# Output weights at sixteen SBUF start addresses modulo 512 bytes, in a kernel bound by TensorE

## The chip, the core and the metric

The kernel runs on one core of a Trainium2 chip. The metric is the device time of one execution in microseconds (us), as the median of several runs. Beside it stands one execution recorded by the hardware profiler; its span runs from the first to the last instruction.

## What is computed

Three blocks follow each other: attention with a causal mask and a cumulative bias (4 x 8 heads, 576 positions, head size 64), a gated product block, and a feed-forward block. The change touches the last one, on 2304 tokens:

```python
def _moe2_ref(x, w_in, w_out) -> np.ndarray:   # x 2304x512, w_in 512x2048, w_out 2048x512
    h = x @ w_in
    g = h - np.tanh(h)
    return (g @ w_out).astype(np.float32)
```

## The kernel before

The kernel keeps the accuracy of wide operands by splitting each one in two float32r tiles, a high part (names that end in h) and a low part (names in l). A product is then three matmuls: high by high, high by low, low by high.

All work is first written down as operations with their tiles, and a planner (`Plan`) puts them in an order by their assumed durations and priorities; tiles are then placed in pools on the left or the right side of SBUF, in the order in which they are listed. A tile that lies over one that was released waits for that tile's last users, and for no others. The planner knows nothing of addresses.

The last stage works through the tokens in five blocks `HT` of 512 columns (the last has 256). For each block and each of sixteen groups f of 128 hidden features it does the following:

- L945: twelve matmuls, weights `wih` and `wil`, moving operand `x2b`, up to 512 columns, into a PSUM bank.
- L953 to L960: ScalarE (ACT) and VectorE (DVE) make g from it, in `u`, `sq`, `th`, `pg`, `mk`.
- L396 (DVE) or L395 (ACT) writes the high part `gh`; L401 (GpSimd, POOL) writes the low part `gl`. These lines are those of the helpers `copy` and `sub`.
- L966 to L968: for each 128 tokens n of the block three matmuls that accumulate over f in bank n. The stationary operand (the weight that is loaded into the array) is a 128-column piece of `gh` or `gl`; the moving operand is the whole of `voh[f]`, `vol[f]`, `voh[f]`, 512 columns each.

`voh[f]` and `vol[f]` are the two parts of 128 rows of `w_out`, one pair for each f, 2048 bytes per partition and tile. The first four pairs are in pool `pre`, on the left behind `wih` and `wil`; their values come back from DRAM by a DMA (`fetch`, tile `wt_d`), while the stage before still runs. The other twelve pairs are in pool `p2`, on the right, and are made by `convert`: DMA into `wraw`, some steps on ACT and DVE in `wt`, a copy into `voh` and a subtraction into `vol`. `p2` lies over the tiles of the stage before: `wah`, `wal`, `woh`, `wol`, the input ring `cf`, and `x2s`, from which that stage's result is stored to DRAM and read back as `x2b`.

In the built program all the large tiles of this stage start at 480 modulo 512 bytes: `wih`, `wil`, `x2b`, `gh`, `gl`, and every `voh` and `vol`. In the attention stage the tiles `kh`, `kl` and `qs`, `q2` start at 480 or 224, and a piece that begins at column 288 of `kh` or `kl` therefore at 96 or 352.

Of the kernel before, what the change touches and what calls it, by code (L numbers as in the profile page):

```python
# [10 lines left out]
F32R = mybir.dt.float32r  # L11
# [5 lines left out]
P = 128  # L17
# [3 lines left out]
DM, DF, DF2 = 512, 1024, 2048  # L21
KC = DM // P
NF = DF // P
NF2 = DF2 // P
# [307 lines left out]
def tile_kernel(ctx, tc, qk, v, s, w1, w2, w3t, w_out, w_in, w_out2, out):  # L332
    nc = tc.nc
# [35 lines left out]
    bank = []  # L369
# [21 lines left out]
    def dma(dst, src, nbytes, r, w, prio, row=4096, issue=450.0, rate=320.0):  # L391
        pl.op([("SP", issue, lambda: nc.sync.dma_start(dst(), src()))], r=r, w=w, prio=prio, xfer=max(nbytes / rate, nbytes / row * 4.0))

    def copy(dst, src, n, r, w, prio, psum=False):
        pl.op([("ACT", c_act(n, psum), lambda: nc.scalar.activation(dst(), src(), AF.Copy)),  # L395
               ("DVE", c_dve(n, not psum), lambda: nc.vector.tensor_copy(dst(), src()))], r=r, w=w, prio=prio, two=not psum, kind="copy")  # L396
# [7 lines left out]
    def split(hi, hb, lo, lb, src, n, r, prio, psum=False):  # L404
        copy(hi, src, n, r, [hb], prio, psum)
        sub(lo, src, hi, n, r + [hb], [lb], prio, psum)
# [7 lines left out]
    def pe(mms, fn, r, w, prio):  # L414
        pl.op([("PE", c_mms(mms), fn)], r=r, w=w, prio=prio, mms=mms)
# [58 lines left out]
    NPRE = PARAM["npre"]  # L474
    pre = Pool("pre", "left")
    p2 = Pool("p2", "right")
    voh = [(pre if f < NPRE else p2).buf(f"voh{f}", [P, DM], F32R) for f in range(NF2)]
    vol = [(pre if f < NPRE else p2).buf(f"vol{f}", [P, DM], F32R) for f in range(NF2)]
    x2b = [q_.buf(f"x2b{i}", [P, 2, KC, BLK], F32R) for i, q_ in enumerate((pre, p2))]
    gh_r = p2.ring("gh", PARAM["ng"], [P, BLK], F32R)  # L480
    gl_r = p2.ring("gl", PARAM["ng"], [P, BLK], F32R)
# [8 lines left out]
    def assemble(src, prio, first=None, after=()):  # L490
        r_, t_ = raw_r.next(), t1_r.next()
        h32, l32 = (lambda: r_.t[:, :, 1]), (lambda: r_.t[:, :, 0])
        tf = lambda: t_.t.bitcast(F32)
        dma(lambda: r_.t, lambda: src.bitcast(U32).rearrange("p (n t) -> p n t", t=2), P * 4096, list(after), [r_], prio if first is None else first)
        pl.op([("ACT", c_act(512), lambda: nc.scalar.activation(tf(), h32().bitcast(F32), AF.Abs)),  # L495
               ("DVE", c_dve(512, True), lambda: nc.vector.tensor_scalar(t_.t, h32(), 0x7FFFFFFF, None, op0=ALU.bitwise_and))], r=[r_], w=[t_], prio=prio, two=True, kind="copy")
        dve(lambda: nc.vector.tensor_scalar(tf(), tf(), HI_CLAMP, LO_CLAMP, op0=ALU.min, op1=ALU.max), 512, [t_], [t_], prio, fast=True)
        dve(lambda: nc.vector.tensor_scalar(t_.t, t_.t, 3, 0x3FFFFFF8, op0=ALU.logical_shift_left, op1=ALU.bitwise_and),
            512, [t_], [t_], prio, fast=True)
        dve(lambda: nc.vector.scalar_tensor_tensor(t_.t, h32(), 0xC0000000, t_.t, op0=ALU.bitwise_and, op1=ALU.bitwise_or),  # L500
            512, [r_, t_], [t_], prio, two=True)
        dve(lambda: nc.vector.scalar_tensor_tensor(t_.t, l32(), 29, t_.t, op0=ALU.logical_shift_right, op1=ALU.bitwise_or),
            512, [r_, t_], [t_], prio, two=True)
        return t_

    def convert(src, hi, hb, lo, lb, prio, first=None, after=()):
        t_ = assemble(src, prio, first, after)
        split(hi, hb, lo, lb, lambda: t_.t.bitcast(F32), 512, [t_], prio)
# [5 lines left out]
    def fetch(i, hi, hb, lo, lb, prio, first=None):  # L514
        dma(lambda: lo().bitcast(F32), lambda: wt_d.t[i], P * 2048, [(wt_d, i)], [lb], prio if first is None else first)
        copy(hi, lambda: lo().bitcast(F32), 512, [lb], [hb], prio)
        sub(lo, lambda: lo().bitcast(F32), hi, 512, [hb], [lb], prio)
# [60 lines left out]
    for e in e2[:1] + [None] + e2[1:]:  # L578
        if e is None:
            zero([lambda: ssum.t], [20], [ssum], -5, 1.0)  # L580
            for R in rqk:
                a = 0 if R is rqk[0] else S
# [8 lines left out]
    for t, (q0, q1) in enumerate(QT):  # L591
        a, o = ROFF[t]
# [331 lines left out]
    raw_r.bufs, t1_r.bufs = raw[:2], bit[:2]  # L924
    for f in range(NF2):
        if f in lay:
            fetch(f, lambda f=f: voh[f].t, voh[f], lambda f=f: vol[f].t, vol[f], 3.5e5 + 10 * f, PARAM["layf"])
        else:
            convert(w_out2[f * P:(f + 1) * P, :], lambda f=f: voh[f].t, voh[f], lambda f=f: vol[f].t, vol[f], 3.5e5 + 10 * f)
    h_ring = Ring(bank[BLK // P:8])  # L930
    for j, (t0, t1) in enumerate(HT):
        w = t1 - t0
        X2 = x2b[j % 2]
        js = range(t0 // 512, (t1 - 1) // 512 + 1)
        dma(lambda X2=X2, w=w: X2.t[:, :, :, :w].bitcast(F32), lambda t0=t0, t1=t1: x2_d.t[:, :, :, t0:t1], P * 8 * w * 4,
            [(x2_d, [i * KC + d for i in js for d in range(KC)])], [X2], 3.0e5)
        for f in range(NF2):
            pos = (j * NF2 + f) * 10.0
            bk = h_ring.next()

            def mm(bk=bk, X2=X2, f=f, w=w):
                a = slice(f * P, (f + 1) * P)
                for k in range(KC):
                    for n, (w_, i) in enumerate(((wih, 0), (wih, 1), (wil, 0))):
                        nc.tensor.matmul(bk.t[:, :w], w_.t[:, k, a], X2.t[:, i, k, :w], start=k == 0 and n == 0, stop=k == KC - 1 and n == 2)  # L945
            parts = [k * 4 + f // 4 for k in range(KC)]
            pe(12 * f_mm(w), mm, [X2, (wih, parts), (wil, parts)], [bk], 2.0e6 + pos)
            u, sq, th, pg, mk = u_r.next(), sq_r.next(), th_r.next(), pg_r.next(), mk_r.next()
            gh, gl = gh_r.next(), gl_r.next()
            hp = lambda bk=bk, w=w: bk.t[:, :w]  # L950
            c_ = lambda x, w=w: x.t[:, :w]
            pr = 3.0e5 + pos
            act(lambda u=u, hp=hp, c_=c_: nc.scalar.activation(c_(u), hp(), AF.Square), w, [bk], [u], pr, psum=True)  # L953
            act(lambda u=u, sq=sq, c_=c_: nc.scalar.activation(c_(sq), c_(u), AF.Square, bias=const.t[:, 0:1], scale=SQ_A), w, [u, const], [sq], pr, extra=93.0)
            act(lambda th=th, hp=hp, c_=c_: nc.scalar.activation(c_(th), hp(), AF.Tanh), w, [bk], [th], pr, psum=True)
            dve(lambda u=u, pg=pg, hp=hp, c_=c_: nc.vector.tensor_tensor(c_(pg), hp(), c_(u), op=ALU.mult), w, [bk, u], [pg], pr)  # L956
            dve(lambda sq=sq, pg=pg, c_=c_: nc.vector.scalar_tensor_tensor(c_(pg), c_(sq), SQ_K, c_(pg), op0=ALU.add, op1=ALU.mult), w, [sq, pg], [pg], pr, two=True)
            act(lambda u=u, mk=mk, c_=c_: nc.scalar.activation(c_(mk), c_(u), AF.Relu, bias=const.t[:, 1:2]), w, [u, const], [mk], pr, extra=93.0)  # L958
            dve(lambda th=th, hp=hp, c_=c_: nc.vector.tensor_tensor(c_(th), hp(), c_(th), op=ALU.subtract), w, [bk, th], [th], pr)
            dve(lambda pg=pg, mk=mk, th=th, c_=c_: nc.vector.copy_predicated(c_(pg), c_(mk).bitcast(U32), c_(th)), w, [mk, th], [pg], pr, two=True)  # L960
            copy(lambda gh=gh, c_=c_: c_(gh), lambda pg=pg, c_=c_: c_(pg), w, [pg], [gh], pr)
            sub(lambda gl=gl, c_=c_: c_(gl), lambda pg=pg, c_=c_: c_(pg), lambda gh=gh, c_=c_: c_(gh), w, [pg, gh], [gl], pr, psum=t1 == NT and f >= NF2 - 2)
            for n in range(w // P):
                def om(n=n, f=f, gh=gh, gl=gl):
                    a = slice(n * P, (n + 1) * P)
                    nc.tensor.matmul(bank[n].t, gh.t[:, a], voh[f].t, start=f == 0, stop=False)  # L966
                    nc.tensor.matmul(bank[n].t, gh.t[:, a], vol[f].t, start=False, stop=False)  # L967
                    nc.tensor.matmul(bank[n].t, gl.t[:, a], voh[f].t, start=False, stop=f == NF2 - 1)  # L968
                pe(3 * f_mm(512), om, [gh, gl, voh[f], vol[f]], [bank[n]], 2.0e6 + pos + PARAM["outlag"] + n)
        for n in range(w // P):  # L970
            ob = osb_r.next()
            for a, z in ((0, 256), (256, 512)) if t1 == NT else ((0, 512),):
                copy(lambda ob=ob, a=a, z=z: ob.t[:, a:z], lambda n=n, a=a, z=z: bank[n].t[:, a:z], z - a, [bank[n]], [(ob, int(a > 0))] if t1 == NT else [ob], 3.0e5 + j * 160, psum=True)
            dma(lambda t0=t0, n=n: out[t0 + n * P:t0 + (n + 1) * P, :], lambda ob=ob: ob.t, P * DM * 4, [ob], [], 0)
# [46 lines left out]
```

## Time and profile before

| | us |
|---|---|
| median of 3 runs | 932.16 (930.49 to 932.52) |
| the profiled execution, its own time | 931.48 |
| its span | 929.8 |
| TensorE (PE) busy | 921.6 |
| DVE busy | 700.5 |
| ACT busy | 426.6 |
| POOL busy | 377.8 |

The execution's own time is 1.7 us longer than the span of its instructions. PE's busy time is made of modelled ends of overlapping matmuls; how long a matmul really holds the engine is read from the distance between the starts of two that follow each other.

### The profile page before, as it was taken

How to read it: one execution, taken by the hardware profiler on the slowest of the kernel's cores; microseconds unless marked ns; L12 is line 12 of the kernel's file. 1: busy time of each engine (PE TensorE's matmuls, PEld its weight loads, DVE VectorE, ACT ScalarE, POOL GpSimd, SP SyncE). 2: the span in 40 equal slices, each digit the busy share in tenths (PEclk: the TensorE clock that was granted, in tenths of full speed). 3: DMA queues.
4: the chain of work that ended last, by engine and by line, in shares of the span. 5: the costliest groups of instructions: out<-in, count | busy, mean ns of one | idle time of the engine just before them, and what ended most of it. 6: DMA issues, size and time to landing. Idle time of an engine off the chain costs nothing.

```text
span 929.8 us, 14217 instructions
## 1 busy us (share of the span) xinstructions
PE 921.6 (99%) x5007; PEld 765.1 (82%) x5007; DVE 700.5 (75%) x1485; ACT 426.6 (46%) x952; POOL 377.8 (41%) x309
## 2 busy tenths in 40 slices
PE   9999999999999999999999999999999999999998
PEld 7777878888887888899888988888888888888887
DVE  8999897876664299996789999997556655656665
ACT  7857565655551022211423275554444444444353
POOL 2256765545342044414978544452222222222221
PEclk9999999999999999999999999999999999999999
DMA  7666646654421144477897652221020001100010
GB/s 226 183 199 181 201 146 205 213 160 135 131 84 49 56 147 155 164 233 240 284 326 247 227 176 68 75 107 46 1 91 15 31 1 46 46 1 0 1 47 23
DMA packets 58888, 115.36 MB, mean 124 GB/s; under 512 B 5713, under 2 KB 24305, under 8 KB 58818
## 3 DMA queue, kind: packets, MB, share of 16 engines
q1 hardware_dynamic: 58818, 114.47, 38.6%
q8 instruction: 39, 0.64, 0.3%
q14 instruction: 31, 0.25, 0.1%
HBM read 85.30 MB, written 25.46 MB: 119 GB/s over the span
## 4 chain that ended last, share of the span: by engine, by line
PE 92%; DVE 4%; POOL 1%; issue 1%; ACT 1%; DMA 1%; POOLq 0%; DVEq 0%
PE bank L945 21%; PE bank L806 20%; PE bank L966 7%; PE bank L967 7%; PE bank L968 7%; PE bank L725 5%; PE bank L752 4%; PE bank L908 4%; PE bank L909 4%; PE bank L907 4%; PE bank L670 2%; PE bank L671 2%; PE bank L668 2%; PE bank L872 1%; PE bank L871 1%; PE bank L870 1%
## 5 line engine op out<-in xcount | busy, mean ns | idle before, releaser
L401 POOL TENSOR_TENSOR gl<-pg,gh 128x512 fp32r<-128x512 f32 (+1 forms) x78 | 99.2, 1272 | 260.9 <-DVE gh L396 249.0
L945 PE MATMUL bank<-x2b,wih 128*128 128x512 f32 (+1 forms) x640 | 181.3, 368 | 0.0
L945 PEld LDWEIGHTS bank<-x2b,wih 128*128 128x128 f32 x640 | 117.0, 188 | 21.2
L958 ACT ACTIVATE mk<-u,const 128x512 f32<-128x512 f32 (+1 forms) x80 | 54.5, 681 | 142.5 <-DVE pg L960 142.4
L945 PE MATMUL bank<-x2b,wil 128*128 128x512 f32 (+1 forms) x320 | 117.7, 368 | 0.0
L966 PE MATMUL bank<-voh,gh 128*128 128x512 f32 x288 | 112.2, 390 | 0.0
L967 PE MATMUL bank<-vol,gh 128*128 128x512 f32 x288 | 112.2, 390 | 0.0
L968 PE MATMUL bank<-voh,gl 128*128 128x512 f32 x288 | 112.0, 389 | 0.0
L691 ACT ACTIVATE e<-e,nmx 128x576 f32<-128x576 f32 (+4 forms) x160 | 89.2, 559 | 39.7 <-DVE nmx L685 38.8
L956 DVE TENSOR_TENSOR pg<-bank,u 128x512 f32<-128x512 f32 (+1 forms) x80 | 50.9, 636 | 42.3 <-POOL gl L401 42.3
L685 DVE CUSTOM_DVE_ANT_0 e<-bank,msk 128x288 f32<-128x288 f32 (+4 forms) x160 | 64.3, 422 | 16.5 <-PE bank L671 14.2
L725 PE MATMUL bank<-ident,e 128*128 128x128 f32 (+1 forms) x480 | 75.4, 276 | 0.6 <-ACT e L691 0.3
L396 DVE CAST gh<-pg 128x512 fp32r<-128x512 f32 (+1 forms) x77 | 30.5, 396 | 52.8 <-PE bank L967 52.6
L945 PEld LDWEIGHTS bank<-x2b,wil 128*128 128x128 f32 x320 | 60.3, 188 | 9.9
L401 POOL TENSOR_TENSOR xl<-cf,xh 128x512 fp32r<-128x512 f32 (+1 forms) x40 | 53.3, 1360 | 34.2 <-DVE xh L396 32.3
L953 ACT ACTIVATE u<-bank 128x512 f32<-128x512 f32 (+1 forms) x80 | 43.7, 546 | 50.4 <-PE bank L945 42.3
L395 ACT ACTIVATE en<-bank 128x256 f32<-128x256 f32 (+3 forms) x97 | 40.9, 427 | 52.2 <-PE bank L725 42.3
L495 ACT ACTIVATE wt<-wraw 128x512 f32<-128x512 f32 x54 | 36.4, 673 | 59.4 <-DMA wraw<-w_in 26.7
L968 PEld LDWEIGHTS bank<-voh,gl 128*128 128x128 f32 x288 | 54.1, 188 | 11.4
L966 PEld LDWEIGHTS bank<-voh,gh 128*128 128x128 f32 x288 | 54.2, 188 | 10.8
L967 PEld LDWEIGHTS bank<-vol,gh 128*128 128x128 f32 x288 | 54.1, 188 | 10.5
L806 PE MATMUL bank<-xh,w1h 128*128 128x512 f32 (+1 forms) x160 | 62.7, 392 | 0.0
(134 smaller groups left out, 2280.2 us busy)
## 6 DMA issues: line engine op xcount, KB each, us to landing
rqk<-qk SPq DMA_DIRECT2D x24, 576.0 KB
wraw<-w_out SPq DMA_DIRECT2D x24, 512.0 KB
wraw<-w SPq DMA_DIRECT2D x16, 512.0 KB
c_d<-cst SPq DMA_DIRECT2D x32, 256.0 KB
wraw<-w3t SPq DMA_DIRECT2D x16, 512.0 KB
wraw<-w_in SPq DMA_DIRECT2D x16, 512.0 KB
cf<-c_d SPq DMA_DIRECT2D x32, 256.0 KB
x_d<-x2s SPq DMA_DIRECT2D x16, 512.0 KB
```

Source lines behind the costliest of these rows:

```text
L401: o.append(("POOL", c_pool2(n), lambda: nc.gpsimd.tensor_tensor(dst(), a(), b().bitcast(F32), op=ALU.subtract)))
L685: nc.vector.tensor_tensor_reduce(e.t[:nq, EOFF[t] + k0:EOFF[t] + k1], bk.t[:nq, :k1 - k0], bi.t[:nq, bo + k0:bo + k1], -0.125, 3.0e38 if f ...
L691: act(lambda: nc.scalar.activation(et(), et(), AF.Exp, bias=nmx.t[:nq, i, tm:tm + 1], scale=-1.0, accum_out=ssum.t[:nq, pj, t, i:i + 1]), ...
L725: nc.tensor.transpose(bk.t[:rows, (at + m) * P:(at + m + 1) * P], e.t[:, EOFF[t] + c * P:EOFF[t] + c * P + rows], ident.t)
L806: nc.tensor.matmul(bk.t[:, :w], w_.t[:, k, f * P:(f + 1) * P], x_.t[:, k, :w], start=k == 0 and i == 0, stop=k == KC - 1 and i == 2)
L945: nc.tensor.matmul(bk.t[:, :w], w_.t[:, k, a], X2.t[:, i, k, :w], start=k == 0 and n == 0, stop=k == KC - 1 and n == 2)
L953: act(lambda u=u, hp=hp, c_=c_: nc.scalar.activation(c_(u), hp(), AF.Square), w, [bk], [u], pr, psum=True)
L956: dve(lambda u=u, pg=pg, hp=hp, c_=c_: nc.vector.tensor_tensor(c_(pg), hp(), c_(u), op=ALU.mult), w, [bk, u], [pg], pr)
L958: act(lambda u=u, mk=mk, c_=c_: nc.scalar.activation(c_(mk), c_(u), AF.Relu, bias=const.t[:, 1:2]), w, [u, const], [mk], pr, extra=93.0)
L966: nc.tensor.matmul(bank[n].t, gh.t[:, a], voh[f].t, start=f == 0, stop=False)
L967: nc.tensor.matmul(bank[n].t, gh.t[:, a], vol[f].t, start=False, stop=False)
L968: nc.tensor.matmul(bank[n].t, gl.t[:, a], voh[f].t, start=False, stop=f == NF2 - 1)
```

## The change

Each of the 32 tiles becomes 128 columns (512 bytes) wider, and its 512 columns of data begin at column 8f, so 32f bytes behind the tile's start. `wo2` makes that view, and all writers and readers use it. `voh[f]` and `vol[f]` have the same f and so the same offset; their data start at 480 + 32f modulo 512: 480 for f = 0, 0 for f = 1, 32 for f = 2, up to 448 for f = 15.

```diff
-    voh = [(pre if f < NPRE else p2).buf(f"voh{f}", [P, DM], F32R) for f in range(NF2)]
-    vol = [(pre if f < NPRE else p2).buf(f"vol{f}", [P, DM], F32R) for f in range(NF2)]
+    voh = [(pre if f < NPRE else p2).buf(f"voh{f}", [P, DM + P], F32R) for f in range(NF2)]
+    vol = [(pre if f < NPRE else p2).buf(f"vol{f}", [P, DM + P], F32R) for f in range(NF2)]
+    wo2 = lambda x, f: x.t[:, 8 * f:8 * f + DM]
...
-            fetch(f, lambda f=f: voh[f].t, voh[f], lambda f=f: vol[f].t, vol[f], 3.5e5 + 10 * f, PARAM["layf"])
+            fetch(f, lambda f=f: wo2(voh[f], f), voh[f], lambda f=f: wo2(vol[f], f), vol[f], 3.5e5 + 10 * f, PARAM["layf"])
...
-            convert(w_out2[f * P:(f + 1) * P, :], lambda f=f: voh[f].t, voh[f], lambda f=f: vol[f].t, vol[f], 3.5e5 + 10 * f)
+            convert(w_out2[f * P:(f + 1) * P, :], lambda f=f: wo2(voh[f], f), voh[f], lambda f=f: wo2(vol[f], f), vol[f], 3.5e5 + 10 * f)
...
-                    nc.tensor.matmul(bank[n].t, gh.t[:, a], voh[f].t, start=f == 0, stop=False)
-                    nc.tensor.matmul(bank[n].t, gh.t[:, a], vol[f].t, start=False, stop=False)
-                    nc.tensor.matmul(bank[n].t, gl.t[:, a], voh[f].t, start=False, stop=f == NF2 - 1)
+                    nc.tensor.matmul(bank[n].t, gh.t[:, a], wo2(voh[f], f), start=f == 0, stop=False)
+                    nc.tensor.matmul(bank[n].t, gh.t[:, a], wo2(vol[f], f), start=False, stop=False)
+                    nc.tensor.matmul(bank[n].t, gl.t[:, a], wo2(voh[f], f), start=False, stop=f == NF2 - 1)
```

The 32 x 512 bytes per partition fill what was free between the two sides: `pre` now ends where `p2` begins. Since the tiles are wider, they lie over other tiles of the stages before, and six instructions wait for other semaphores. The first place is POOL at the start of the last stage, where the first subtractions into `vol` are (numbers behind a name are the program's own; `vol_4970` is `vol4`, `vol_4972` is `vol6`). Before:

```order
L401 TENSOR_TENSOR wil<-wt_89,wih 128x512 [waits DVE_49]
L401 TENSOR_TENSOR vol_4970<-wt_83,voh_4958 128x512 [waits DMAHW4_49,DMAHW1_49,DVE_49]
L401 TENSOR_TENSOR vol_4971<-wt_84,voh_4959 128x512 [waits DVE_49]
L401 TENSOR_TENSOR gl_4986<-pg_4995,gh_4983 128x512 [waits DVE_49,PE_49]
L401 TENSOR_TENSOR gl_4987<-pg_4996,gh_4984 128x512 [waits DVE_49]
L401 TENSOR_TENSOR gl_4988<-pg_4995,gh_4985 128x512 [waits DVE_49]
L401 TENSOR_TENSOR vol_4972<-wt_83,voh_4960 128x512 [waits PE_49,Activation_49]
```

The same rows of the changed program:

```order
L401 TENSOR_TENSOR wil<-wt_89,wih 128x512 [waits DVE_49]
L401 TENSOR_TENSOR vol_4970<-wt_83,voh_4958 128x512 [waits DMAHW3_49,DMAHW5_49,DMAHW2_49,DMAHW7_49,DMAHW1_49,DVE_49]
L401 TENSOR_TENSOR vol_4971<-wt_84,voh_4959 128x512 [waits DVE_49]
L401 TENSOR_TENSOR gl_4986<-pg_4995,gh_4983 128x512 [waits DVE_49,PE_49]
L401 TENSOR_TENSOR gl_4987<-pg_4996,gh_4984 128x512 [waits DVE_49]
L401 TENSOR_TENSOR gl_4988<-pg_4995,gh_4985 128x512 [waits DVE_49]
L401 TENSOR_TENSOR vol_4972<-wt_83,voh_4960 128x512 [waits DMAHW4_49,DMAHW1_49,Activation_49]
```

The order is the same. `vol4` waits for DMAs on five semaphores; DMAHW2 and DMAHW3 stand for the last two stores from `x2s`, and the others for earlier stores from it. `vol6` waits for two stores from `x2s` in place of a matmul. The second place is ACT in the middle of the stage before, where the first four pairs are taken from what `fetch` brought (`voh_4204` is `voh0`). Before:

```order
L395 ACTIVATE x2s_3986<-bank_58 128x512 [waits PE_49]
L395 ACTIVATE voh_4204<-vol_4208 128x512 [waits DMAHW2_49,DMAHW4_49,DMAHW0_49,DVE_49]
L395 ACTIVATE voh_4205<-vol_4209 128x512 [waits DMAHW5_49]
L395 ACTIVATE voh_4206<-vol_4210 128x512 [waits DMAHW6_49]
L395 ACTIVATE voh_4207<-vol_4211 128x512 [waits DMAHW7_49]
```

The same rows of the changed program:

```order
L395 ACTIVATE x2s_3986<-bank_58 128x512 [waits PE_49]
L395 ACTIVATE voh_4204<-vol_4208 128x512 [waits DMAHW4_49,DMAHW2_49,DMAHW5_49,DMAHW0_49,DVE_49]
L395 ACTIVATE voh_4205<-vol_4209 128x512 [waits DMAHW6_49,DMAHW5_49]
L395 ACTIVATE voh_4206<-vol_4210 128x512 [waits DMAHW6_49]
L395 ACTIVATE voh_4207<-vol_4211 128x512 [waits DMAHW7_49]
```

`voh0` and `voh1` each wait for one more DMA, a store of the ring `cst` to DRAM that was issued before the fetch of `vol0`. Nothing else moved.

## Rows read from the trace of the kernel before

**Rows 1.** Page: span, busy time by engine, PE's granted clock in 40 slices.
```profile
span 929.8 us, 14217 instructions
...
PE 921.6 (99%) x5007; PEld 765.1 (82%) x5007; DVE 700.5 (75%) x1485; ACT 426.6 (46%) x952; POOL 377.8 (41%) x309
...
PEclk9999999999999999999999999999999999999999
```
**Rows 2.** Page: the chain that ended last, by engine and by line.
```profile
PE 92%; DVE 4%; POOL 1%; issue 1%; ACT 1%; DMA 1%; POOLq 0%; DVEq 0%
PE bank L945 21%; PE bank L806 20%; PE bank L966 7%; PE bank L967 7%; PE bank L968 7%; PE bank L725 5%; PE bank L752 4%; PE bank L908 4%; PE bank L909 4%; PE bank L907 4%; PE bank L670 2%; PE bank L671 2%; PE bank L668 2%; PE bank L872 1%; PE bank L871 1%; PE bank L870 1%
```
**Rows 3.** The chain in order of time: start us, us, what.
```profile
849.36 2.72 PE bank L945 x12
...
896.40 1.43 PE bank L945 x12
```
**Rows 4.** Timeline of PE: start us, us, engine, line, op, tiles, form, count.
```profile
601.67 0.39 PE L966 MATMUL bank<-voh,gh 128*128 128x512 f32 x1
...
604.39 0.62 PE L945 MATMUL bank<-x2b,wih 128*128 128x512 f32 x2
```
**Rows 5.** Groups by form: count, busy us, mean ns, idle us before.
```profile
L966 PE MATMUL bank<-voh,gh 128*128 128x512 f32 x288 | 112.2, 390 | 0.0
...
L966 PEld LDWEIGHTS bank<-voh,gh 128*128 128x128 f32 x288 | 54.2, 188 | 10.8
```
**Rows 6.** Timeline of POOL at the start of the last stage.
```profile
537.77 1.68 POOL L401 TENSOR_TENSOR vol<-wt,voh 128x512 fp32r<-128x512 f32 x1 [5.10 <-DVE voh L396]
...
542.75 1.61 POOL L401 TENSOR_TENSOR gl<-pg,gh 128x512 fp32r<-128x512 f32 x1 [0.52 <-DVE gh L396]
```
**Rows 7.** Timeline of DVE, the copy into voh4.
```profile
537.27 0.42 DVE L396 CAST voh<-wt 128x512 fp32r<-128x512 f32 x1
```
**Rows 8.** Timeline of SyncE's DMA issues in two stretches.
```profile
440.75 0.43 SPq L392 DMA_DIRECT2D c_d<-cst  x1
...
442.18 1.84 SPq L392 DMA_DIRECT2D vol<-wt_d  x4
...
531.08 3.04 SPq L392 DMA_DIRECT2D x_d<-x2s  x3
```
**Rows 9.** DMA view of 529:537.7: GB/s in 40 equal slices.
```profile
GB/s 264 207 490 414 245 240 254 344 330 184 61 0 151 151 169 377 395 245 132 358 410 316 377 381 377 377 386 306 358 353 316 85 9 38 188 151 113 207 282 301
```
**Rows 10.** Tiles vol and gl: duration ns min/median/max, first and last start us.
```profile
L967 PE MATMUL bank<-vol,gh x288: 389/389/398, 548.9 to 925.1; 128*128 128x512 f32 x144
L401 POOL TENSOR_TENSOR vol<-wt,voh x12: 1287/1441/1736, 537.8 to 623.3; 128x512 fp32r<-128x512 f32 x12
...
L968 PE MATMUL bank<-voh,gl x288: 388/389/389, 549.1 to 925.4; 128*128 128x512 f32 x144
```
**Rows 11.** Timeline of ACT, the first four copies into voh.
```profile
448.03 2.19 ACT L395 ACTIVATE voh<-vol 128x512 fp32r<-128x512 f32 x4
```
**Rows 12.** Groups by form: the multiply on POOL in the attention stage.
```profile
L780 POOL TENSOR_TENSOR xf<-xf,xr 128x512 f32<-128x512 f32 x16 | 20.5, 1284 | 0.3 <-DVE xf L396 0.3
```
**Rows 13.** Timeline of PE, a head of the attention stage.
```profile
215.52 0.30 PE L670 MATMUL bank<-kh,qs 128*128 128x288 f32 x1
215.65 0.30 PE L671 MATMUL bank<-kl,q 74*128 74x288 f32 x1
215.79 0.29 PE L670 MATMUL bank<-kh,qs 128*128 128x288 f32 x1
215.92 0.30 PE L671 MATMUL bank<-kl,q 74*128 74x288 f32 x1
216.06 0.27 PE L725 MATMUL bank<-ident,e 128*128 128x128 f32 x1
```
**Rows 14.** Timeline of PE in the last block, behind matmuls of 256 columns.
```profile
897.67 0.40 PE L966 MATMUL bank<-voh,gh 128*128 128x512 f32 x1
...
898.14 0.39 PE L968 MATMUL bank<-voh,gl 128*128 128x512 f32 x1
```

## The prediction

> **What bounds the kernel now.** I read the head of the page first. [...] Then the chain that ended last, by engine: PE is 92% of it and DMA 1%; the three matmul lines that read the changed tiles (L966 to L968) are 21% of it, as much as L945 alone [rows 2]. So only two things can move the time here: how long one matmul occupies PE, or a wait so late that PE runs dry.
>
> The chain in order of time shows how even the last stage is. Twelve matmuls of L945 with 512 columns take 2.72 us, so 226.7 ns each [rows 3]; some fifty such rows follow each other. The matmuls that read `voh` and `vol` keep the same pace: the starts of twelve of them, from 601.67 to the L945 at 604.39, also span 2.72 us, and the engine is never idle ahead of one [rows 4, 5]. Their durations of 390 ns are modelled ends that overlap; the pace is the distance between starts. There are 288 on each of the three lines, 864 in all [rows 5], 864 x 0.2267 = 195.9 us of PE time. That is all the work whose operand addresses the change touches on PE.
>
> **The change, part by part.**
>
> *Instructions.* No instruction is added, removed or moved on any engine apart from waits: the excerpts from the order above show POOL and ACT before and after, and PE, DVE and SP stand as they did, waits included. Columns, partitions, element counts and bytes per transfer are the same; the 128 added columns of each tile are never written or read. Instruction count: 0 us.
>
> *Waits.* Wider tiles lie over other released tiles, so six instructions wait for something else. Only one of them looks close. The subtraction that writes `vol4` now waits for the last stores of `x2s` where it waited for older ones. It starts at 537.77 [rows 6]. What held it until then was the DVE copy into `voh4`, started at 537.27 and 0.42 us long, so done at 537.69 [rows 7]. The last of the `x2s` stores were issued by 531.08 + 3.04 = 534.12 [rows 8]. In the DMA row of 529 to 537.7, slices of 0.22 us, the traffic falls to 85, 9 and 38 GB/s at about 535.7 to 536.4 and then starts again, with the next loads [rows 9]. I take the stores as landed there, which leaves about 1.3 us before 537.69: cost 0. The cover is that DVE copy. If it were gone and the stores landed late, `vol5` and then the first `gl` (542.75) would queue behind on POOL [rows 6], but PE reads the first `vol` at 548.9 and the first `gl` at 549.1 [rows 10], and that `gl` is done at 542.75 + 1.61 = 544.36, so a delay of up to 4.7 us is still free. Bound: 0 to 0. On ACT, `voh0` and `voh1` wait in addition for two stores of `cst`; `cst` was last stored at 440.75, in front of the fetch of `vol` at 442.18 that these copies wait for in any case, and ACT starts them at 448.03 [rows 8, 11]. `vol6`, `voh9` and `voh12` drop a wait or wait for an older transfer: 0.
>
> *Writes to the new addresses.* 16 copies, 16 subtractions and 4 fetches now write at starts 32 bytes apart. The trace has no tile write at each of these residues. The nearest rows: the POOL multiply of L780, whose tiles start at 128 or 384 modulo 512, takes 1284 ns for 128x512 [rows 12], and the subtraction into `vol`, at 480, takes 1287 at its fastest [rows 10]: no difference between a multiple of 64 bytes and one that is 32 off. Even 10% on all twelve later ones (0.14 us each, 1.7 us) would fall on an engine that is busy 377.8 of 929.8 us [rows 1], against tiles that are written some microseconds ahead of their use. 0 us.
>
> *Reads by PE.* This is the one term that the trace doesn't settle. All full-width moving operands of the last stage start at 480 modulo 512 now, and so do the weights `gh` and `gl`, column blocks of 512 bytes. After it, `voh` and `vol` start at 480 + 32f, so 15 of 16 pairs change. What rows show of other starts: in the attention stage moving operands of 288 columns begin at 96 (two matmuls), then at 480 (two), with weights at 224, and the starts are 0.13, 0.14, 0.13 and 0.14 us apart [rows 13]. Within the 0.01 us that such a row resolves, it is the same. But all are odd multiples of 32, and for an even f the new starts stay of that kind (480, 32, 96, ...); an odd f gives 0, 64, 128, ..., of which no matmul of this type in the trace tells anything. Value taken: 0, by these rows. From both sides: a matmul of 256 columns takes 1.43 us / 12 = 119.2 ns [rows 3], so two of them 238.3 and one of 512 columns 226.7: each carries a part of 11.7 ns that doesn't grow with the columns. Were that part due to where the operands lie, the most to win is 11.7 ns on 15/16 x 864 = 810 matmuls, 9.5 us. On the other side, the same line with the same operand is at times slower: after L945 with 256 columns the first and the third of them start at 897.67 and 898.14, 235 ns for each of two, 8.3 over the normal pace [rows 14]. As a price for a less lucky start that is 810 x 8.3 ns = 6.7 us.
>
> [...]
>
> Sum: 0 + 0 + 0 + 0. The profiled execution took 931.48 us, 0.7 under the median of 932.16 (runs from 930.49 to 932.52); with no term in the sum the forecast lies between them, 932.0.
>
> **The rivals.**
>
> *A read stall goes away (faster).* Weight loads run beside the matmuls, 188 ns each [rows 5], from tiles with the same residue as the moving operand. If they collide there, other starts would part them. For it: the 11.7 ns per matmul is there, and I can't say what it is. Against it: in [rows 13] the two operands start 256 or 128 bytes apart modulo 512, and the pace doesn't show it. Times: 932.0 - 9.5 = 922.5 if 15 of 16 pairs win all of it; 932.0 - 5.1 = 926.9 if only the odd f do (432 x 11.7 ns), since they alone start at a multiple of 64 bytes.
>
> *A read stall appears (slower).* The place is L966 to L968: one operand of each matmul leaves the common residue, or begins at one at which reads take longer. For it: equal residues everywhere could be the good case. Against it: again [rows 13]. Price 8.3 ns on 810 matmuls: 932.0 + 6.7 = 938.7. It decides from 1.9 us / 810 = 2.3 ns per matmul on.
>
> *The new waits hold POOL.* It would take a delay over 4.7 us at 537.77 to reach PE; a store issued by 534.12 would have to land after 542. I give it 1 in 100, inside slower.
>
> **How the numbers follow.** A measurement of this kernel can tell about 0.2%, 1.9 us, from no change. No change: 0.79. A stall gone: 0.12, of which a part may be smaller than either price. A stall or a wait more: 0.09. The forecast's own case holds the time within 0.2%, 930.1 to 933.9; the three runs already spread by 2.0 us, and a part of either rival could show as a fraction, so I open the range by some 0.6 us on both sides: 929.5 to 934.5. That leaves out the full prices on either side.
>
> **What would show it.** If I am right, L966 to L968 keep starts 226.7 ns apart for every f, with the twelve of one f in 2.72 us, as long as L945's twelve; the granted clock stays full; POOL's subtraction for `vol4` starts within 0.1 us of the end of the DVE copy into `voh4`. If the first rival is right, the twelve matmuls of an odd f, or of each f but one, take near 2.58 us while L945's still take 2.72; under the second they take up to 2.82. I would be wrong in the argument, even with the right time, if the pace differed between one f and the next.

## The result and the profile after

| | before | changed |
|---|---|---|
| median | 931.89 us (4 runs, 930.49 to 932.52) | 936.67 us (4 runs, 935.94 to 936.97) |
| ratio, 95% interval | | 1.0052 (1.0035 to 1.007) |
| span of the profiled execution | 929.8 us | 934.8 us |

The change makes the kernel 4.8 us slower, 0.5%. Of all executions in this document, two stand far apart, one of 1865 us (`pad_only`) and one of 4184 us (`left_only`), and no figure below holds them. Head of the page of the changed kernel (its lines are one higher than before: L946 was L945, L967 to L969 were L966 to L968):

```profile
span 934.8 us, 14219 instructions
...
PE 926.8 (99%) x5007; PEld 765.0 (82%) x5007; DVE 701.1 (75%) x1485; ACT 425.9 (46%) x952; POOL 375.5 (40%) x309
...
PEclk9999999999999999999999999999999999999999
```

The two instructions more are semaphore waits on POOL. PE has 5.2 us more than in [rows 1] with the same 5007 matmuls and the same granted clock (a mean of 1.000 in both); DVE and ACT have what they had. So the time went into single matmuls, and the groups by form say into which:

```profile
L946 PE MATMUL bank<-x2b,wih 128*128 128x512 f32 x512 | 158.5, 391 | 0.0
...
L967 PE MATMUL bank<-voh,gh 128*128 128x512 f32 x288 | 113.6, 395 | 0.0
...
L969 PE MATMUL bank<-voh,gl 128*128 128x512 f32 x288 | 113.6, 394 | 0.0
L968 PE MATMUL bank<-vol,gh 128*128 128x512 f32 x288 | 113.5, 394 | 0.0
```

The same groups of the kernel before, beside L966 in [rows 5]:

```profile
L945 PE MATMUL bank<-x2b,wih 128*128 128x512 f32 x512 | 157.7, 389 | 0.0
...
L967 PE MATMUL bank<-vol,gh 128*128 128x512 f32 x288 | 112.2, 390 | 0.0
L968 PE MATMUL bank<-voh,gl 128*128 128x512 f32 x288 | 112.0, 389 | 0.0
```

The three lines that read the changed tiles took 4 to 5 ns more each, idle time none as before. A turn of twelve shows it in the distance of starts. Such a turn holds the last six matmuls of one f and the first six of the next, here f = 11 and 12, and not the twelve of one f of which the prediction speaks. Timeline of PE in the changed kernel; the last line is the first matmul of L946 behind them:

```profile
701.39 0.40 PE L967 MATMUL bank<-voh,gh 128*128 128x512 f32 x1
701.63 0.40 PE L968 MATMUL bank<-vol,gh 128*128 128x512 f32 x1
701.86 0.40 PE L969 MATMUL bank<-voh,gl 128*128 128x512 f32 x1
...
704.19 0.62 PE L946 MATMUL bank<-x2b,wih 128*128 128x512 f32 x2
```

Twelve take 2.80 us, where [rows 4] had 2.72. And L946, whose operands lie at the same residues (starts modulo 256 bytes) as before, has lost its uniform 2.72 us of [rows 3] in the chain in order of time:

```profile
825.91 2.75 PE bank L946 x12
831.45 2.76 PE bank L946 x12
837.01 2.72 PE bank L946 x12
```

Taken over the whole trace, the mean distance from one start to the next, over 54 matmuls for each f (in the kernel before: 226.7 to 227.7 for every f):

```
start of voh[f], vol[f], modulo 256      224    0     32    64    96    128   160   192
f = 0 to 7,  ns                         228.1 233.8 230.6 234.3 231.8 233.5 233.3 233.1
f = 8 to 15, ns                         229.0 233.8 230.8 234.3 231.8 233.4 233.1 232.9
```

The pattern repeats after 256 bytes within 0.9 ns, and only f = 0 and f = 8, 256 bytes apart, keep nearly the old pace. The mean over all f is 232.3 ns against 227.2, so 864 x 5.2 ns = 4.5 us; L946 goes from 226.7 to 228.3 on 709 distances, 1.1 us. Together 5.6 us, and that is what the last stage grew by. Its first matmuls on the timelines of PE, before and after:

```profile
532.29 0.63 PE L945 MATMUL bank<-x2b,wih 128*128 128x512 f32 x2
```

```profile
531.72 0.63 PE L946 MATMUL bank<-x2b,wih 128*128 128x512 f32 x2
```

To the end of the span the stage lasts 397.5 us before and 403.1 us after; ahead of it, the second execution happened to be 0.6 us quicker.

### The profile page after: what moved, and what is told of

The parts are those of the page before. It is cut to its first block, busy times and chain, and to the rows that moved or that the text cites. A ratio compares the mean times of both kernels' runs of the same rounds, so it can differ in the third digit from the quotient of the medians.

```text
span 934.8 us, 14219 instructions
## 1 busy us (share of the span) xinstructions
PE 926.8 (99%) x5007; PEld 765.0 (82%) x5007; DVE 701.1 (75%) x1485; ACT 425.9 (46%) x952; POOL 375.5 (40%) x309
## 4 chain that ended last, share of the span: by engine, by line
PE 94%; DVE 4%; POOL 1%; DMA 1%; ACT 0%; issue 0%; POOLq 0%; DVEq 0%
PE bank L946 21%; PE bank L807 20%; PE bank L967 7%; PE bank L969 7%; PE bank L968 7%; PE bank L726 5%; PE bank L753 4%; PE bank L908 4%; PE bank L909 4%; PE bank L910 4%; PE bank L671 2%; PE bank L672 2%; PE bank L871 2%; PE bank L872 2%; PE bank L873 2%; PE bank L669 1%
## 5 line engine op out<-in xcount | busy, mean ns | idle before, releaser
L946 PE MATMUL bank<-x2b,wih 128*128 128x512 f32 (+1 forms) x640 | 182.1, 369 | 0.0
L946 PEld LDWEIGHTS bank<-x2b,wih 128*128 128x128 f32 x640 | 117.0, 188 | 22.8
L946 PE MATMUL bank<-x2b,wil 128*128 128x512 f32 (+1 forms) x320 | 117.8, 368 | 0.0
L967 PE MATMUL bank<-voh,gh 128*128 128x512 f32 x288 | 113.6, 395 | 0.0
L969 PE MATMUL bank<-voh,gl 128*128 128x512 f32 x288 | 113.6, 394 | 0.0
L968 PE MATMUL bank<-vol,gh 128*128 128x512 f32 x288 | 113.5, 394 | 0.0
L946 PEld LDWEIGHTS bank<-x2b,wil 128*128 128x128 f32 x320 | 60.3, 188 | 10.3
L503 DVE SCALAR_TENSOR_TENSOR wt<-wraw,wt 128x512 uint32<-128x512 uint32 x72 | 64.9, 904 | 0.2
L969 PEld LDWEIGHTS bank<-voh,gl 128*128 128x128 f32 x288 | 54.1, 188 | 12.8
L967 PEld LDWEIGHTS bank<-voh,gh 128*128 128x128 f32 x288 | 54.2, 188 | 11.7
L968 PEld LDWEIGHTS bank<-vol,gh 128*128 128x128 f32 x288 | 54.1, 188 | 11.8
```

The costliest lines, as they stand in the source:

```text
L967: nc.tensor.matmul(bank[n].t, gh.t[:, a], wo2(voh[f], f), start=f == 0, stop=False)
L968: nc.tensor.matmul(bank[n].t, gh.t[:, a], wo2(vol[f], f), start=False, stop=False)
L969: nc.tensor.matmul(bank[n].t, gl.t[:, a], wo2(voh[f], f), start=False, stop=f == NF2 - 1)
```

## The experiments

Two theories stood at the start. **The own start:** where the moving operand begins decides its pace. **The difference:** the moving operand and the weights that are loaded beside it, for the next matmul, hinder each other, by the distance of their starts modulo 256 bytes. That a load runs beside the matmul ahead of its own is seen on the timeline of the loads of the kernel before: the load for L967 starts 0.01 us behind the L966 of [rows 4].

```profile
601.68 0.19 PEld L967 LDWEIGHTS bank<-vol,gh 128*128 128x128 f32 x1
```

A third theory was that the wider tiles or the new waits cost the time. All comparisons are with runs of the kernel before on the same chip (930.8 us).

**The width alone** (`pad_only`). Every use of the tiles goes through the two views.

```diff
-    voh = [... .buf(f"voh{f}", [P, DM], F32R) ...]     (vol alike)
+    voh = [... .buf(f"voh{f}", [P, DM + P], F32R) ...]
+    voh_, vol_ = (lambda f: voh[f].t[:, 0:0 + DM]), (lambda f: vol[f].t[:, 0:0 + DM])
```

> The 32 tiles are 128 columns wider as in the change, with the same new waits, but the data start at column 0, so at 480 modulo 512 as before. If the loss comes from where PE's operands start (either by the difference of the two operands' starts or by the moving operand's own start): 931.9 us, within 1 us, and L966 to L968 at 226.7 ns between starts. If it comes from the wider tiles, their new neighbours or the new waits: 936.7 us.

Measured 930.94 us, ratio 1.0005 (0.9995 to 1.0015). Its groups by form have the durations of [rows 5] again:

```profile
L967 PE MATMUL bank<-voh,gh 128*128 128x512 f32 x288 | 112.2, 390 | 0.0
L968 PE MATMUL bank<-vol,gh 128*128 128x512 f32 x288 | 112.2, 390 | 0.0
```

Width, neighbours and waits cost nothing that can be measured.

**Steps of 256 bytes** (`step256`): as `pad_only`, with the views at `64 * (f % 2)`.

> As the change, but the data of odd f start 256 bytes behind the tile's start and those of even f at it. If starts count modulo 256 bytes, as f = 0 and f = 8 of the changed kernel suggest (227 to 230 ns, all others 230 to 235): 931.9 us, pace 226.7 ns for all f. If they count modulo 512 bytes and f = 8 is a chance: about half the loss, 934.3 us, odd f at 230 ns or more.

Measured 930.94 us, ratio 1.0006 (0.9997 to 1.0015), 227.2 ns for nearly every f, where 32 bytes had made 233.8 in the changed kernel. In this kernel starts count modulo 256 bytes.

**The weights move, not the moving operand** (`stat_shift`).

```diff
-    gh_r = p2.ring("gh", PARAM["ng"], [P, BLK], F32R)     (gl_r alike)
+    gh_r = p2.ring("gh", PARAM["ng"], [P, BLK + 64], F32R)
...
+            go = 8 * (f % 8)      (gh and gl are written and read from column go on)
```

> voh and vol stay at 480; only gh and gl, the weights, move to 480 + 32(f mod 8). Theory of the difference: slower by as much as the change, 936.5 us, paces of 230 to 235 ns where f mod 8 is not 0. Theory of the moving operand's own start: 931.9 us, pace 226.7 ns.

Measured 936.40 us, ratio 1.0067 (1.0052 to 1.0082). `voh` and `vol` lie as before, and yet their matmuls are slow by the groups:

```profile
L968 PE MATMUL bank<-voh,gh 128*128 128x512 f32 x288 | 113.7, 395 | 0.0
L970 PE MATMUL bank<-voh,gl 128*128 128x512 f32 x288 | 113.5, 394 | 0.0
L969 PE MATMUL bank<-vol,gh 128*128 128x512 f32 x288 | 113.4, 394 | 0.0
```

By f 232 to 233.5 ns, but 228.8 and 229.9 at f = 0 and 8, and 230.5 and 230.8 at f = 6 and 14, whose weights lie at 160. There the moving operand starts 64 bytes on, and the changed kernel had its lowest value behind f = 0 and 8, 230.6, at f = 2, where the moving operand minus the weights is likewise 64. The own start is refuted. At each difference taken with its sign, the two kernels agree within 1.1 ns; taken with the other sign, they are up to 2.8 ns apart. No run has the wider `gh` and `gl` without the shift; the near-even pace at f = 0 and 8 speaks against a cost of the width.

**Both move together** (`both_shift`): the views of `pad_only` and `go`, both at `8 * (f % 8)`.

> voh and vol start at 480 + 32(f mod 8), and gh and gl of the same f are written and read at the same offset, so both operands of a matmul start at the same residue modulo 256. Theory of the difference (a weight load and the moving operand beside it hinder each other by the distance of their starts modulo 256): within 1.5 us of 931.9, a little above it at most, since at the two ends of a group of twelve the weights loaded are those of L945 at the old residue; pace near 227 ns inside the group. Theory of the own start (the moving operand's residue alone): 936.7 us, paces of 230 to 235 ns for f that are not multiples of 8.

Measured 934.69 us, ratio 1.0045 (1.003 to 1.006), 3.9 us more than before: over the 1.5 us that the difference allowed at most, and under what the own start said. Of the six matmuls of one f in a turn all but the last agree with the load beside them, and still the distances are 228.9 to 231.2 ns. So the difference of the one load beside it is not all that a matmul feels.

**All of the left side moves** (`left_only`, and `left_again`, the same kernel once more, for its profile). Only the first columns of `neg` are used.

```diff
-    neg = keep.buf("neg", [3 * NH, 80])
+    neg = keep.buf("neg", [3 * NH, 8])
```

> The tiles of before, but a small tile at the head of the left side is 288 bytes narrower, so everything on the left starts 32 bytes lower modulo 256 (192 in place of 224) and the right side stays. No wait differs from before. Theory of the difference: slow in places that the change never touched: L806 (weights left, moving operand right, difference 32, 768 matmuls of 512 columns at some 6 ns), L945 in the blocks whose x2b is on the right (384), and L966 to L968 for f = 0 to 3 (216): about 8 to 11 us over before. Theory of the moving operand's own start: only x2b on the left (three of five blocks) and f = 0 to 3 lie elsewhere, about 4 us over before.

> The kernel left_only once more, for its profile. Theory of the difference: L806 with 512 columns (weights at 192, moving operand at 224) at 230 to 235 ns; L907 to L909 (both on the right) at 226.7 once they are clear of other matmuls; L945 at 226.7 or returning to it in the blocks whose x2b is on the left (192 as its weights), at 230 or more in the blocks whose x2b is on the right. Time 938.5 us. Any theory that looks at one operand alone puts the slow lines elsewhere: L907 to L909 and L806 have the same moving residue and would be equal.

`left_only` measured 938.3 us, ratio 1.0081 (1.0064 to 1.0097), `left_again` 939.75 in its one execution. A narrower constant makes a kernel 7.5 us slower whose instructions and waits are otherwise those of before; the difference had said 8 to 11, the own start about 4. The chain in order of time of the kernel before, and then of `left_again`, has the same long piece of L806, in the gated block:

```profile
291.75 60.76 PE bank L806 x267
```

```profile
292.09 62.49 PE bank L806 x267
```

That is 227.6 and 234.0 ns each. In the same kernel L907 to L909, which read the same tiles `xh` and `xl` at the same place but with weights from the right side, go on at 226.7 (timeline of `left_again`, nine from the first to the last line):

```profile
479.74 0.39 PE L907 MATMUL bank<-xh,wah 128*128 128x512 f32 x1
...
481.78 0.39 PE L907 MATMUL bank<-xh,wah 128*128 128x512 f32 x1
```

One moving operand, two paces, by the weights it goes with. L945 splits as expected too: 233.2 ns where `x2b` is on the right, 228.2 where it is on the left.

**Everything moves** (`both_sides`): `left_only`, and eight columns more at the upper end of the right side.

```diff
+    p2.buf("pad_p2", [P, 8])
+    xp.buf("pad_xp", [P, 8])
```

> As left_only, and the right side 32 bytes lower too, so all the large tiles start at 192 modulo 256 in place of 224 and their differences are as before (only the identity matrix of the transposes stays where it was). Theory of the difference: as before, within 1.5 us. Theory of the own start: 192 is one of the slow residues of the changed kernel (233 ns at f = 7), now for some 3000 matmuls of 512 columns: 15 us or more over before.

Measured 930.36 us, ratio 0.9995 (0.9985 to 1.0004). The residue itself, 224 or 192, is of no account. From the first matmul of the last stage to the end of the span, `pad_only`, `step256` and `both_sides` take 397.6 us each in their profiles, where the kernel before took 397.5.

**One offset for all f** (`both_const`): as `both_shift`, both offsets 24 columns for every f.

> voh, vol, gh and gl all start 96 bytes further (64 modulo 256), for every f, while x2b, wih and wil stay. Both operands of L966 to L968 agree; only where L945 and they follow each other does a matmul run beside a load of the other residue. Theory of the difference with a slow return to the old pace after a disturbance: of twelve matmuls the first six at 229 to 233 ns, the last ones near 227; in all 2 to 4 us over before. Theory of the own start: all twelve at 233 or 234 ns, as f = 3 and f = 11 of the changed kernel, 6 us over before.

Measured 937.11 us, ratio 1.0068 (1.0051 to 1.0085): more than the change itself, though only two matmuls in 24 run beside a load of another residue. The difference had said 2 to 4 us, and by the time alone the 6 us of the own start came true. The trace shows another pace than the own start's twelve at 233 or 234 ns. Timeline of PE where L971 hands over to L946:

```profile
721.07 0.40 PE L971 MATMUL bank<-voh,gl 128*128 128x512 f32 x1
721.31 0.63 PE L946 MATMUL bank<-x2b,wih 128*128 128x512 f32 x2
721.77 0.40 PE L946 MATMUL bank<-x2b,wil 128*128 128x512 f32 x1
722.01 0.62 PE L946 MATMUL bank<-x2b,wih 128*128 128x512 f32 x2
722.46 0.40 PE L946 MATMUL bank<-x2b,wil 128*128 128x512 f32 x1
722.70 0.62 PE L946 MATMUL bank<-x2b,wih 128*128 128x512 f32 x2
723.16 0.39 PE L946 MATMUL bank<-x2b,wil 128*128 128x512 f32 x1
723.39 0.61 PE L946 MATMUL bank<-x2b,wih 128*128 128x512 f32 x2
723.84 0.39 PE L946 MATMUL bank<-x2b,wil 128*128 128x512 f32 x1
724.07 0.40 PE L969 MATMUL bank<-voh,gh 128*128 128x512 f32 x1
```

Twelve matmuls of L946 take 2.76 us although the operands of all but the last agree with the load beside them. Averaged by their place in the group of twelve (59 groups of L946, 64 to 75 of L969 to L971), and L946 of the changed kernel beside it:

```
place                       1     2     3     4     5     6     7     8     9     10    11    12
both_const, L946          229.2 233.2 235.6 224.5 230.8 235.7 228.2 232.4 230.7 226.3 226.7 228.2
both_const, L969 to L971  235.2 233.0 235.3 226.7 229.4 235.4 229.4 232.0 231.2 227.0 226.5 236.8
changed,    L946          229.7 232.8 229.1 229.3 229.3 227.7 226.9 227.3 227.2 226.7 226.6 226.7
```

After one pair of differing residues the pace is uneven for about nine matmuls and then even again, and L946, whose moving operand stayed where it was, pays as well. In the second row place 12 is slow at 236.8 ns: that matmul's own two operands agree, and only the weights loaded beside it, those of the next L946, lie at another residue. A group of twelve loses 41 ns in the first row and 58 in the second against 12 x 226.7; 59 x 0.041 + 64 x 0.058 = 6.1 us, and the time rose by 6.3. In `both_shift` a new difference comes after every six matmuls of L969 to L971, so they hardly ever become even: 3.1 ns more on 863 distances and 1.4 on 709 of L946 make 3.6 of the 3.9 us.

**Finer steps** (`fine16`, `fine4`): the views of `pad_only` at `4 * f` and at `f` columns.

> voh and vol start 16f bytes behind 224 modulo 256, so steps of 16 bytes over one whole period. Theory of the difference: f = 0 near 227 to 229 ns, even f as in the changed kernel at the same offset (f = 2 like its f = 1, 234), odd f in the same band of 230 to 236. A start below 226 ns for any f would say that there is a better distance than none; I expect none.

> voh and vol start 4f bytes behind 224 modulo 256: steps of one column, 0 to 60 bytes. If only whole lines of 16 bytes count: f = 0 to 3 near 227 to 229 ns, and groups of four equal f from there on (f = 4 to 7 like the 231.6 of 16 bytes, f = 8 to 11 like the 233.2 of 32). If every byte of difference counts: f = 1 to 3 already at 230 or more. No pace below 226 ns expected.

```
fine16, 16f bytes, f = 0 to 15, ns  227.2 231.6 233.2 232.7 230.7 231.7 234.7 230.0 232.5 233.0 233.5 232.4 233.1 234.5 232.7 232.5
fine4,   4f bytes, f = 0 to 15, ns  228.4 236.1 233.8 229.6 231.3 237.2 233.0 227.6 233.4 235.6 233.9 229.9 232.8 234.0 231.8 228.3
```

936.72 and 938.67 us in one execution each; of the 7.9 us that `fine4` has over before, 5.9 lie in the last stage (403.4 us) and the rest ahead of it. Since unevenness lasts over some nine matmuls, each figure holds a part of its neighbour's. `fine16` gives at each multiple of 32 bytes within 1 ns what the changed kernel gave. `fine4` refutes the lines of 16 bytes: four bytes cost more than sixteen (236.1 ns against 231.6 in `fine16`). Two of its distances, 28 and 60 bytes, are nearly as good as none (227.6 and 228.3). No distance that was tried is better than none, which has 227.2 in `fine16`.

**The other way round** (`aligned`).

```diff
-    ident = keep.buf("ident", [P, P])
     const = keep.buf("const", [P, 4])
-    neg = keep.buf("neg", [3 * NH, 80])
+    neg = keep.buf("neg", [3 * NH, 16])
+    ident = keep.buf("ident", [P, P])
...
+    att.buf("pad_a", [P, 24])
     en = [att.buf(f"en{i}", [P, ETOT], n=5) for i in range(2)]
...
+    att.buf("pad_b", [P, 40])
```

> The kernel before, with the tiles of the attention stage that do not start at 224 modulo 256 moved there: the identity matrix (its place among the constants changed) and en, by two small tiles, and all others kept at 224. Nothing of the change. Theory of the difference: fewer disturbed matmuls in that stage; all of what L806 loses there against its even pace is 1.2 us, so 0 to 1.5 us faster than before. If only float32r matmuls count, or the stage is disturbed by its changing shapes anyway: no difference, within 0.5 us.

Measured 930.31 us, ratio 0.9997 (0.9988 to 1.0006); L806 at 228.6 ns where it had 228.8. No gain. The author's two guesses, that the change of shapes breaks the even pace in that stage anyway, or that the plain float32 matmuls of those tiles don't count, are shown by no run.

## Why the prediction was wrong

**What bounds the kernel** was right: PE alone, busy 926.8 of 934.8 us after the change too, and only the length of a matmul or a late wait could move the time.

**Waits and writes at 0** were right. In the changed kernel POOL's subtraction for `vol4` starts right behind the DVE copy into `voh4` (timeline of POOL, then of DVE, ended at 536.71 + 0.42 = 537.13), after the same idle 5.10 us as in [rows 6]:

```profile
537.20 1.68 POOL L401 TENSOR_TENSOR vol<-wt,voh 128x512 fp32r<-128x512 f32 x1 [5.10 <-DVE voh L396]
```

```profile
536.71 0.42 DVE L396 CAST voh<-wt 128x512 fp32r<-128x512 f32 x1
```

`pad_only` shows the same of the waits by the time. As to the writes, the fastest subtraction into `vol` takes 1287 ns in the changed kernel too, as in [rows 10].

**The term "Reads by PE", "Value taken: 0, by these rows"**, is the step that failed; it cost 5.6 us in the profiled stage. The sign that the prediction named for it, a pace that differs between one f and the next, is what came. The rows could not carry the 0. Two of the four matmuls in [rows 13] start at 480 beside weights at 224, which by `step256` is no difference at all. A pair of equal starts stands there for two matmuls, and `both_const` shows that a pace needs nine to become even; and the loss, 4 to 8 ns at most f, is less than the 10 ns that such a row resolves. More to the point, in the trace of before every full-width float32r matmul has its two operands at one residue. Its 226.7 ns were the price of that case, and no row showed a full-width matmul in any other. The prediction saw this ("equal residues everywhere could be the good case") and gave it, as the rival "a read stall appears", together with the new waits, 0.09. That rival happened, with the mechanism as named, one operand leaving the common residue. Its size was near by accident: 8.3 ns on 810 matmuls, 6.7 us, against 5.2 ns on 864 and 1.6 on L945, which the rival left out. The 8.3 came from [rows 14], where the pace is uneven behind matmuls of 256 columns; that this is the same unevenness by another cause is not shown.

**"A read stall goes away"** did not happen, and no start in 16 steps of 32, 16 or 4 bytes brought the average of an f below the 226.7 ns of before: the lowest is 228.1 in the changed kernel, 227.2 in `fine16` and 227.6 in `fine4`. None of the 11.7 ns per matmul that the prediction took as the most to win was won by a placement that was tried. Nor does the moving operand set the pace alone: weights that move alone slow the matmuls of an operand that stays, 227.2 to 232.2 ns in `stat_shift` and 227.6 to 234.0 in `left_again`.

What stays open is the inner cause: why a period of 256 bytes, why 28 and 60 bytes (227.6 and 228.3 ns) are nearly harmless, and what it is that takes nine matmuls to come back. That the two reads meet in SBUF is argued from which operand moves, not seen.

## What to carry to other kernels

Where PE runs float32r matmuls back to back, here 512 columns with new weights for each, lay the moving operands and the weights at the same start modulo 256 bytes (here 226.7 to 227.7 ns for each f, against 230.6 to 234.3 at the other residues of the change), and look at the built program's addresses for it: one small constant 288 bytes narrower at the head of one side cost this kernel 0.8%. A pace that is the same on every row of a trace may be that of one lucky layout; before costing a change of layout at nothing, ask whether any row shows another. Groups of matmuls on different residues should not alternate in short turns, since each hand-over cost 41 and 58 ns over about nine matmuls in `both_const`, at 96 bytes of difference.

## What was not expected of the hardware

A single pair of operands at different residues leaves a trace of nine matmuls, 224 to 237 ns in `both_const`, in an order that repeats from group to group (over the groups of L946 the standard deviation at a place is 0.4 to 1.3 ns). Four bytes of difference (236.1 ns in `fine4`) are worse than sixteen (231.6 in `fine16`), while 28 (227.6) nearly equal none (227.2 in `fine16`).
